# Written-out orders for TensorE, ScalarE and VectorE over the first part of an attention-and-MoE kernel, four masks moved to ScalarE, and shorter zero products

## The chip, the cores and the metric

One core of a Trainium2 chip runs the kernel. The metric is the device time of one execution in microseconds (us), the median of several runs. The engines are TensorE (PE; PEld is its weight load), VectorE (DVE), ScalarE (ACT), GpSimd (POOL), and the DMA queues, of which SyncE (SP) and POOL issue the ones that matter here.

## The reference

Three layers follow one another on 3072 tokens of 256 features (4 batches, 768 positions).

```python
# 1. a chunked linear attention with decay, 4 batches, 8 heads, width 32, state 16
log_a = np.log(np.clip(a, 1e-06, 1.0))
...
    L = np.exp(cum[:, :, :, None] - cum[:, :, None, :])
    L = L * causal
    CB = np.einsum('bhin,bhjn->bhij', Cc, Bc)
    M = CB * L
    y_intra = np.einsum('bhij,bhjd->bhid', M, xc)
    y_inter = np.einsum('bhin,bhnd->bhid', Cc, state) * decay_to_i[:, :, :, None]
    state = decay_full[:, :, None, None] * state + np.sum(Bx, axis=2)
# 2. a norm over the features and a gated layer, d_ff = 1536
rms = np.sqrt(np.mean(x * x, axis=-1, keepdims=True) + 1e-06)
xn = x / rms * rms_g
g = xn @ w_gate
silu = g * (1.0 / (1.0 + np.exp(-g)))
val = xn @ w_val
x = silu * val @ w_out
# 3. a second layer, d_ff = 2048
h = x @ w_in
g = h * np.clip(h + 3.0, 0.0, 6.0) / 6.0
out = g @ w_out
```

## The kernel before

The attention is cut into 24 chunks, numbered k, of 128 positions of one batch; chunks 4j to 4j+3 are one group of 512 tokens. Each chunk is worked in two halves of 64. The products of layers 2 and 3 are made from a high and a low part of each factor (names ending in h and l), as three products each.

Every piece of work is an operation of a planner (class `Plan`): it has a planned duration on one engine or more, keys that it reads and writes, and often a name (tag). `Plan.run` lays the operations out in planned time as a list scheduler does and then issues the instructions in that order. `P.chain(engine, names)` forces the named operations of an engine into the order given; what is not named goes where the planner puts it. Waits between the engines come from the data that the issued instructions touch. At the end `P.fill` looks at the planned time of TensorE between two named operations (`visit1` and `h010`) and puts zero products (`idle`, 128x256 in f32) into each gap that is longer than a product (430 ns) and `SLACK`.

The front is the work on the first 4 chunks. Its steps, with the names that the lists use (a number after a name is a chunk k, or a pair q of chunks):

- `heat`, `zero`, `warm`: products of zeros on TensorE. `sp`, `px` spread the decay over the partitions (bank tiles Q).
- `scan`: VectorE makes the decay matrix L of a chunk. `bh`, `ch`: VectorE scales B and C. `P`: ScalarE copies the prefix products out of PSUM.
- `sc`, `gr`: TensorE makes the scores and the state products of a chunk in a PSUM tile `sps`, one for chunks 0 and 1, another for 2 and 3.
- `SM`: VectorE multiplies scores and L. `um`: the state product times a mask of zeros and ones. `V`: VectorE makes the state at the end of the chunk.
- `visit0`, `visit1`: TensorE makes the attention's result of two chunks from `SM`, `um` and `ch` in the same `sps` tile.
- `sq`, `ev`: ScalarE squares and copies that result. `mn`: TensorE sums the squares. `rt` (ScalarE), `v`, `iv`, `nw` (VectorE): the inverse root. `bk`: TensorE spreads it. `sx`: VectorE scales. `xh` (ScalarE), `xl` (VectorE): high and low part of the normed input for layer 2.

After the front come the weights of layer 2, block f of 12: a load on SP's queue into one of six buffers, `wa` and `wb` (ScalarE), `wj` (VectorE; when it is done the buffer's next load can be issued), `wh` (high part, either engine) and `wl` (low part, VectorE).

Layer 2 itself runs in steps i: `h` (TensorE, hidden products; `h000` to `h111` are those of the first two blocks, cut into halves of 256 tokens and named by block, half, gate or value; from step 4 on they are `h4:0`, `h4:1`, ...), `s` (ScalarE, silu), `m` (VectorE, times the value), `g` (ScalarE, high part), `l` (VectorE, low part) and `r` (TensorE, the result). `h010` is the first product of the second half and needs `xl1`. The later chunks are visited between these steps (`visit2None`, `visit32`, ...: the pair that begins, the pair that ends). For them POOL issues loads of L, of `cb` (chunk data) and of P; the first of these is held back by a one-element copy (`hold`, L499) that reads the result of `nw0`.

Products after the front are recorded under line L970 (function `mm3`), most VectorE products under L289 (`two`).

## Time and profile before

| | |
|---|---|
| median of 3 runs | 596.59 us (595.4 to 598.26) |
| the profiled execution | 595.57 us |
| its span, first to last instruction | 593.8 us |
| TensorE, weight load, VectorE, ScalarE, GpSimd busy | 585.7, 474.0, 471.7, 370.9, 35.5 us |
| granted TensorE clock over the span | 0.998 |

Times within the profile are counted from the first instruction. Matmuls are pipelined and their recorded durations overlap, so that what a product costs in a row of products is the distance between two starts; the same holds for the other engines, where a next instruction can start shortly before the recorded end of the one ahead. A row of the timeline merges neighbouring instructions of one kind (xN).

### The profile page before, as it was taken

The page shows a single profiled execution, that of the slowest core. Times are in us where ns is not written, and L with a number is a line of the kernel's source. Part 1 is how long each engine was busy: PE and PEld are TensorE (multiplying, and loading weights), DVE is VectorE, ACT ScalarE, POOL GpSimd, SP SyncE. Part 2 cuts the span into 40 slices and gives each one's busy share as a digit, 9 for nine tenths or more (in the row PEclk, how much of TensorE's full clock was granted, in tenths as well). Part 3 has the DMA queues.
Part 4 walks back from the last instruction along what each step waited for, and adds up shares of the span by engine and source line. Part 5 has one row for each costly group of instructions (what it writes and reads, how often), then busy time and mean ns, then how long its engine had stood idle before and what let it go on. Part 6 is the DMA issues. An engine that isn't in the chain of part 4 may idle for free.

```text
span 593.8 us, 10861 instructions
## 1 busy us (share of the span) xinstructions
PE 585.7 (99%) x4352; PEld 474.0 (80%) x4352; DVE 471.7 (79%) x870; ACT 370.9 (62%) x654; POOL 35.5 (6%) x64
## 2 busy tenths in 40 slices
PE   9999999999999999999999999999999999999997
PEld 6787878788778778877787778888888888888885
DVE  8999967947885597899999898787975759775665
ACT  3898523323433363677767787777876668776663
POOL 2403013003210000000000000000000000000000
PEclk9999999999999999999999999999999999999999
DMA  8996104305430111022020101200000000100001
GB/s 329 352 316 179 48 22 143 116 9 150 128 128 19 43 49 63 8 72 71 1 71 2 71 2 71 72 1 1 36 36 1 0 1 1 72 0 1 0 1 71
DMA packets 11130, 40.90 MB, mean 69 GB/s; under 512 B 2484, under 2 KB 3208, under 8 KB 10056
## 3 DMA queue, kind: packets, MB, share of 16 engines
q1 hardware_dynamic: 6312, 23.25, 10.8%
q0 software_dynamic: 4000, 15.74, 9.0%
q10 hardware_dynamic: 768, 1.22, 0.6%
q8 instruction: 34, 0.56, 0.4%
q14 instruction: 16, 0.13, 0.1%
HBM read 36.84 MB, written 3.35 MB: 68 GB/s over the span
## 4 chain that ended last, share of the span: by engine, by line
PE 85%; DVE 8%; DMA 3%; ACT 2%; issue 1%; ACTq 0%; DVEq 0%; SPq 0%
PE hps L970 57%; PE acc L970 23%; PE sps L588 1%; DVE unit L289 1%; PE sps L562 1%; DVE st L289 1%; DMA cb<-comb 1%; PE sps L598 1%; DMA raw<-w 1%; DVE gl L289 1%; DMA rb<-rnd 1%; DVE p L289 1%; PE sps L573 1%; DVE w1t L289 0%; DVE raw L1209 0%
## 5 line engine op out<-in xcount | busy, mean ns | idle before, releaser
L970 PE MATMUL hps<-xh,w1t 128*128 128x512 f32 (+1 forms) x544 | 146.5, 387 | 0.3 <-ACT p L999 0.2
L970 PEld LDWEIGHTS hps<-xh,w1t 128*128 128x128 f32 x544 | 99.4, 188 | 22.3 <-ACT unit L1472 0.8
L970 PE MATMUL hps<-xl,w1t 128*128 128x512 f32 (+1 forms) x380 | 108.9, 385 | 0.0
L970 PE MATMUL hps<-unit,w1t 128*128 128x512 f32 x324 | 90.2, 389 | 0.0
L970 PE MATMUL acc<-gh,w1t 128*128 128x512 f32 (+1 forms) x288 | 87.9, 387 | 0.0
L970 PEld LDWEIGHTS hps<-xl,w1t 128*128 128x128 f32 x380 | 70.8, 188 | 14.5
L970 PEld LDWEIGHTS hps<-unit,w1t 128*128 128x128 f32 x324 | 60.8, 188 | 12.7
L289 DVE TENSOR_TENSOR gl<-p,gh 128x512 fp32r<-128x512 f32 (+1 forms) x86 | 57.6, 674 | 13.3 <-ACT gh L1007 7.0
L970 PEld LDWEIGHTS acc<-gh,w1t 128*128 128x128 f32 x288 | 53.0, 188 | 11.3 <-issue 0.6
L1007 ACT CAST gh<-p 128x512 fp32r<-128x512 f32 (+1 forms) x50 | 30.2, 605 | 49.2 <-PE acc L970 48.6
L970 PE MATMUL acc<-gl,w1t 128*128 128x512 f32 (+1 forms) x158 | 60.7, 384 | 0.0
L1314 ACT ACTIVATE p<-hps,half 128x512 f32<-128x512 f32 x48 | 33.0, 688 | 34.2 <-PE hps L970 34.1
L289 DVE TENSOR_TENSOR unit<-hps,unit 128x512 f32<-128x512 f32 x36 | 24.8, 689 | 35.6 <-PE hps L970 35.6
L999 ACT ACTIVATE p<-hps 128x512 f32<-128x512 f32 (+1 forms) x50 | 29.0, 579 | 36.6 <-DVE gl L289 22.5
L1003 DVE TENSOR_TENSOR p<-p,hps 128x512 f32<-128x512 f32 (+1 forms) x50 | 33.0, 660 | 22.3 <-PE hps L970 20.3
L970 PE MATMUL acc<-unit,w1t 128*128 128x512 f32 x142 | 42.8, 390 | 0.0
L1317 DVE SCALAR_TENSOR_TENSOR p<-p,hps 128x512 f32<-128x512 f32 x48 | 32.9, 686 | 10.8 <-ACT p L1314 10.5
L1321 ACT CAST unit<-p 128x512 fp32r<-128x512 f32 x48 | 29.6, 620 | 8.9 <-DVE p L1317 7.4
L1314 ACT ACTIVATE p<-unit,half 128x512 f32<-128x512 f32 x48 | 34.6, 720 | 0.9 <-DVE unit L289 0.4
L970 PEld LDWEIGHTS acc<-gl,w1t 128*128 128x128 f32 x158 | 29.7, 188 | 6.1
L1321 ACT CAST gh<-p 128x512 fp32r<-128x512 f32 x48 | 29.5, 619 | 7.2 <-DVE p L1317 6.4
L1317 DVE SCALAR_TENSOR_TENSOR p<-p,unit 128x512 f32<-128x512 f32 x48 | 33.0, 689 | 0.8 <-ACT p L1314 0.3
(185 smaller groups left out, 960.6 us busy)
## 6 DMA issues: line engine op xcount, KB each, us to landing
cb<-comb POOLq DMA_DIRECT2D x10, 896.0 KB, 5.6
raw<-w SPq DMA_DIRECT2D x8, 1024.0 KB, 4.8
L<-azero POOLq DMA_DIRECT2D x20, 256.0 KB, 4.5
yT<-w SPq DMA_DIRECT2D x6, 768.0 KB, 8.5
rawx<-w SPq DMA_DIRECT2D x6, 768.0 KB, 9.7
out<-yT SPq DMA_DIRECT2D x10, 256.0 KB, 2.0
P<-pref POOLq DMA_DIRECT2D x20, 64.0 KB, 2.5
rb<-rnd SPq DMA_DIRECT2D x5, 256.0 KB, 3.0
```

The lines of the kernel that those rows point to most:

```text
L289: eng[e].tensor_tensor(out=out, in0=a, in1=b, op=op)
L562: pe.matmul(out=o[64 * c:64 * c + 64, p ^ c], lhsT=cb[r, BN + c * SC:BN + (c + 1) * SC], rhs=cb[r, CP + c * CH:CP + (c + 1) * CH], start=T ...
L573: m = pe.matmul(out=o[32 * p:32 * p + 32, c], lhsT=b[r, s:s + 32], rhs=cb[r, XX + 64 * p:XX + 64 * p + 64], start=False, stop=True, skip_g ...
L588: pe.matmul(out=part(k, Y)[32 * g:32 * g + 32, 2 * t + c], rhs=T["SM", k][r, h ^ 2 * c], lhsT=T["cb", k][r, XX + D * h:XX + D * h + D], st ...
L598: ms.append(pe.matmul(out=y[u % 2 * 64:u % 2 * 64 + 64, u // 2 * 2 + n], lhsT=before(k, c)[r, :], rhs=T["ch", k][r, SC * n:SC * n + SC], s ...
L970: pe.matmul(out=o, lhsT=a, rhs=c, start=first and i == 0, stop=last and i == len(seq) - 1, skip_group_check=skip)
L999: act.activation(out=p[:, :n], in_=hcols(0), func=AF.Silu)
L1003: dve.tensor_tensor(out=p, in0=p, in1=hcols(1), op=ALU.mult)
L1007: act.copy(out=t[:, :n], in_=T["p", i][:, :n])
L1314: act.activation(out=unit(pk), in_=h(), func=AF.Relu, scale=1.0 / 6.0, bias=half)
L1317: dve.scalar_tensor_tensor(out=unit(pk), in0=unit(pk), scalar=1.0, in1=h(), op0=ALU.min, op1=ALU.mult)
L1321: P.op({"ACT": a1(512) + 20}, lambda e: act.copy(out=unit(gk), in_=unit(pk)), r=[pk], w=[gk])
```

## The change

- The written orders of TensorE, ScalarE and VectorE are replaced. The old lists end at `h101`, `xh11` and `xl1`; the new ones go on to `h14:0`, `s13` and `m13`, that is through the whole first group of 512 tokens of layer 2. Many operations get a name for it, and nothing else.
- The masks `um0` to `um3` (four VectorE instructions, one for each chunk) become `um0` and `um2`, one operation for each pair of chunks, on ScalarE (two instructions each, Copy with a scale for each partition), as those of chunks 4 to 7 were already. `um0` is planned after the start of `SM0`.
- `zero` and `warm` are 256 columns and not 512. `SLACK` is 450 and not 150 ns.
- `wh0` goes from ScalarE to VectorE, `wh1` stays on ScalarE, `wh2` stays on VectorE (by the lists).
- `guess`, the first step of the inverse root of the later groups, is one VectorE instruction and not two.
- Some planned durations are changed (`v`, `iv`, `nw`, `bk`, `warm`, `zero`), which only the planner reads.

```diff
-    SLACK, BIAS = 150, 600
+    SLACK, BIAS = 450, 600
...
     def warm(e):
-        pe.matmul(out=T["ps", 0][:, 0], lhsT=zero, rhs=four(zero), start=True, stop=True)
+        pe.matmul(out=T["ps", 0][:, 0, :256], lhsT=zero, rhs=four(zero, 2), start=True, stop=True)
...
-        P.op({"PE": 800}, lambda e: pe.matmul(out=Q[0], lhsT=zero, rhs=four(zero), start=True,
+        P.op({"PE": 430}, lambda e: pe.matmul(out=Q[0][:, :256], lhsT=zero, rhs=four(zero, 2), start=True,
                                               stop=True), w=[("z", 0)], tag="zero")
...
-        if k < B or last:
+        if last:
             P.op({"DVE": d1(64 * n)}, mask, r=[("Su", k // 2, k % 2), ("cs", 0)],
-                 w=[("um", k)] + ([("V1", k)] if k < B else []), boost=bst, ps=held(k),
-                 tag=f"um{k}")
+                 w=[("um", k)], boost=bst, ps=held(k), tag=f"um{k}")
         elif k % 2 == 0:
-            P.op({"ACT": 2 * a1(128)} if k < 2 * B and UMA else {"DVE": d1(256)}, mask2, r=[("Su", k // 2, i) for i in range(2)] + [("cs", 0)],
-                 w=[("um", i) for i in ks], boost=bst, ps=held(k), tag=f"um{k}")
+            P.op({"ACT": 2 * a1(128)} if k < 2 * B else {"DVE": d1(256)}, mask2,
+                 r=[("Su", k // 2, i) for i in range(2)] + [("cs", 0)],
+                 w=[("um", i) for i in ks] + [("V1", i) for i in ks if k < B],
+                 boost=bst, ps=held(k), tag=f"um{k}",
+                 seq=[("SM", i) for i in ks[:1] if k == 0])
...
     def guess(j, a, b):
         v, y, z = (t[:, a:b] for t in rn(j))
-        dve.tensor_scalar(out=z.bitcast(I32), in0=v.bitcast(I32), scalar1=1, scalar2=None,
-                          op0=ALU.logical_shift_right)
-        dve.tensor_scalar(out=y.bitcast(I32), in0=z.bitcast(I32), scalar1=-1.0,
+        dve.tensor_scalar(out=y.bitcast(I32), in0=v.bitcast(I32), scalar1=-0.5,
                           scalar2=float(0x5F3759DF), op0=ALU.mult, op1=ALU.add)
...
-    P.chain("DVE", "spot0 spot1 spot2 spot3 clip each prefix scan0 bh0 scan1 bh1 ch0 ch1 SM0 SM1 um0 "
-            "um1 scan2 scan3 bh2 bh3 ch2 ch3 wj0 v0 iv0 nw0 SM2 SM3 um2 um3 sx00 sx01 wl0 xl0 wj1 "
-            "v1 iv1 nw1 wj2 sx10 sx11 wl1 xl1")
-    P.chain("ACT", "P0 P1 wa0 wb0 sq0 sq1 wa1 rt0 ev0 ev1 wh0 wb1 wa2 xh00 xh01 sq2 sq3 wb2 rt1 ev2 ev3 "
-            "wh1 silu xh10 xh11")
-    P.chain("PE", "heat sp0 sp1 sc0 sc1 px gr0 gr1 sp2 sp3 visit0 zero mn0 mn1 sc2 sc3 gr2 gr3 bk0 warm visit1 "
-            "mn2 mn3 h000 bk1 h001 h100 h101")
+    P.chain("PE", "heat sp0 sp1 sc0 sc1 px sp2 gr0 gr1 sp3 visit0 zero sc3 sc2 gr3 gr2 mn0 mn1 bk0 warm "
+            "visit1 mn3 mn2 h000 bk1 h001 h100 h101 h010 h011 h110 h111 r0 h4:0 r1 h4:1 r2 visit2None "
+            "r3 h5:0 h5:1 r4 h6:0 h6:1 h7:0 h7:1 visit32 h8:0 r5 h8:1 r6 visitNone3 h9:0 h9:1 n1t "
+            "h10:0 h10:1 h11:0 r7 h11:1 r8 h12:0 h12:1 r9 h13:0 r10 h13:1 h14:0")
+    P.chain("ACT", "P0 P1 um0 wb0 wa0 sq0 sq1 wa1 wb1 rt0 ev0 ev1 um2 wa2 wh1 xh01 sq2 sq3 xh00 wb2 rt1 ev2 "
+            "ev3 silu xh11 s0 xh10 wb3 s1 g0 wb4 s2 g1 wa3 g2 s3 wa4 wa5 g3 wh3 s4 wb5 wh4 um4 g4 wb6 "
...
+    P.chain("DVE", "spot0 spot1 spot2 spot3 clip each prefix scan0 bh0 scan1 ch0 bh1 ch1 ch2 ch3 SM0 SM1 "
+            "scan2 scan3 V0 bh2 bh3 V1 wj0 SM2 SM3 v0 iv0 nw0 wj1 V2 wh0 sx01 sx00 wl1 wl0 xl0 v1 iv1 "
+            "nw1 wj2 V3 sx11 sx10 wh2 m0 xl1 wl2 m1 l0 scan5 m2 l1 scan4 m3 l2 wj3 wj4 bh4 l3 wl3 ch4 "
+            "m4 wj5 wl4 l4 U4 SM4 m5 wl5 wj6 scan7 m6 scan6 U5 bh6 V4 wj7 V5 wl6 m7 l5 wl7 U6 U7 V6 "
...
```

## Rows read from the trace of the kernel before

**Rows 1.** Windows, busy time of each engine; last columns: granted clock, DMA share, GB/s
```profile
9.39:25.71 16.32, 15.22 (x305) 11.72 (x289) 15.86 (x41) 13.13 (x27) 5.23 (x9) 1.00 1.03 374
25.71:590.00 564.29, 562.52 (x3978) 457.13 (x3978) 448.14 (x807) 355.48 (x624) 26.80 (x43) 1.00 0.17 55
```

**Rows 2.** Timeline of TensorE, from the first visit to the first product of the second half
```profile
11.40 0.86 PE L588 MATMUL sps<-SM,cb 64*32 64x64 f32 x64
...
21.07 0.73 PE L970 MATMUL hps<-xh,w1t 128*128 128x256 f32 x4
...
21.86 1.46 PE L390 MATMUL acc<-zero 128*128 128x256 f32 x6
23.16 0.61 PE L756 MATMUL sps<-eye,y 128*128 128x128 f32 x4
...
26.26 0.64 PE L970 MATMUL hps<-xh,w1t 128*128 128x256 f32 x4
...
26.98 0.28 PE L970 MATMUL hps<-xh,w1t 128*128 128x256 f32 x1
```

**Rows 3.** Timeline of VectorE over the same stretch
```profile
9.39 0.36 DVE L289 TENSOR_TENSOR ch<-cb,P 128x64 f32<-128x64 f32 x2 [0.26 <-ACT P L293]
9.67 1.28 DVE L619 TENSOR_TENSOR SM<-sps,L 128x512 f32<-128x512 f32 x2
10.87 0.48 DVE L626 TENSOR_TENSOR um<-sps,gs 128x128 f32<-128x128 f32 x2
11.26 2.33 DVE L511 TENSOR_TENSOR_SCAN L<-spread,eye 128x512 f32<-128x512 f32 x2
13.51 0.47 DVE L289 TENSOR_TENSOR bh<-cb,L 128x128 f32<-128x128 f32 x2
...
14.16 0.95 DVE L892 SCALAR_TENSOR_TENSOR yT<-yT 128x768 int32<-128x768 int32 x1
15.03 0.47 DVE L634 SCALAR_TENSOR_TENSOR V<-um,P 128x64 f32<-128x64 f32 x2
15.42 0.15 DVE L744 TENSOR_SCALAR v<-sps 128x2 f32<-128x2 f32 x1
...
23.37 0.56 DVE L295 CAST w1t<-fold 128x768 fp32r<-128x768 f32 x1
23.88 0.87 DVE L761 SCALAR_TENSOR_TENSOR xT<-xT,gs,sps 128x256 f32<-128x256 f32 x2
24.67 0.95 DVE L289 TENSOR_TENSOR w1t<-yT,w1t 128x768 fp32r<-128x768 f32 x1
25.71 0.69 DVE L289 TENSOR_TENSOR xl<-xT,xh 128x512 fp32r<-128x512 f32 x1
26.32 0.41 DVE L1003 TENSOR_TENSOR p<-p,hps 128x256 f32<-128x256 f32 x1
26.65 0.95 DVE L289 TENSOR_TENSOR w1t<-fold,w1t 128x768 fp32r<-128x768 f32 x1
```

**Rows 4.** Timeline of ScalarE at the mask of chunks 6 and 7
```profile
48.39 0.63 ACT L648 ACTIVATE um<-sps,gs 128x128 f32<-128x128 f32 x2 [0.23 <-DVE SM L639]
```

**Rows 5.** Windows around TensorE's idle time before `bk0`, and at the end of the program
```profile
14.43:16.38 1.95, 1.00 (x65) 0.70 (x65) 1.84 (x9) 1.04 (x4) 0.09 (x1) 1.00 1.02 426
588.00:592.00 4.00, 1.93 (x9) 1.27 (x7) 2.14 (x4) 0.74 (x2) 0.00 (x0) 1.00 0.62 230
592.00:594.00 2.00, 0.00 (x0) 0.00 (x0) 0.00 (x0) 0.00 (x0) 0.00 (x0) 0.50 0.19 64
```

**Rows 6.** Timeline of GpSimd and of SyncE's queue: loads of L, loads of weights
```profile
16.83 1.23 POOL L461 DMA_DIRECT2D L<-azero  x2 [0.35 <-POOL L L499]
15.14 8.60 SPq L901 DMA_DIRECT2D yT<-w  x3
```

**Rows 7.** Those two loads of L: issue to landing
```profile
DMA to landing us min/median/max: 8.6/9.1/9.6
```

**Rows 8.** DMA issues on the page: KB of one, us to landing
```profile
yT<-w SPq DMA_DIRECT2D x6, 768.0 KB, 8.5
```

## The prediction

> **What bounds the kernel now.** I read the windows first [rows 1]. From 25.71 us to 590.00 TensorE is busy for 562.52 of 564.29 us: all that its waits can still give back in this whole stretch is 1.77 us. In the front, from 9.39 to 25.71, VectorE is busy for 15.86 of 16.32 us and TensorE for 15.22, but a part of the latter is zero products. So the end of the program is set by the moment from which TensorE has products of layer 2 without a break, and that moment is set by VectorE. The products after it are the same in both kernels.

> The timeline of TensorE [rows 2] shows where that moment is. `h000` begins at 21.07, then come three zero products, `bk1` at 23.16, `h001`, two zero products, `h100`, which needs `wl1` (24.67 and 0.95 long [rows 3]), `h101` at 26.26 and `h010` at 26.98. A hidden product of 256 columns is six records, 0.72 us in all (26.26 to 26.98). From `h010` on the row is dense. `h010` needs `xl1`, and `xl1` begins at 25.71 and takes 0.69 [rows 3]. I therefore follow VectorE's queue from `ch0` (9.39, where it has waited 0.26 for ScalarE's `P0`, which the change leaves where it is) to `xl1`.

> **The change part by part: VectorE's queue.** The costs are distances between starts [rows 3].

> - Four masks leave: two in a row cost 11.26 - 10.87 = 0.39, so four 0.78. Gain.
> - `bh1` used to run while VectorE waited for `P0`; now it stands behind `ch0`. Two `bh` cost 13.89 - 13.51 = 0.38 with the `ch` at 13.89 following, one 0.19. Loss.
> - `wh0` comes from ScalarE. The cast at 23.37 is the same form, and 23.88 - 23.37 = 0.51. Loss.
> - `m0` now stands ahead of `xl1`: 26.65 - 26.32 = 0.33. Loss.
> - `SM0` must wait for `gr1`, and TensorE now makes `sp2` ahead of it. `sp2` is four records of 128x256 in f32; six such records of zeros took 23.16 - 21.86 = 1.30 [rows 2], so four 0.87. Before, `gr1` was done at about 9.6 (`SM0` began at 9.67). Now that is 10.5. VectorE arrives at 9.39 + 0.19 + four `ch` at 0.14 (0.28 for two, 9.39 to 9.67) = 10.14. Wait 0.37. Loss.
> - The old waits of the stretch: 16.32 - 15.86 = 0.46 idle [rows 1]. Some 0.2 of it lies between the short dependent instructions of the two inverse roots and stays; 0.26 goes. Gain.

> Sum: -0.78 + 0.19 + 0.51 + 0.33 + 0.37 - 0.26 = +0.36. `xl1` begins at 26.07 and ends at 26.76, later than before. Yet `h010` can follow at 26.8, since `wl1` and `wl0` are now both ahead of `xl0`, so that the four products `h000` to `h101` (2.88 us and `bk1`) no longer wait for `wl1` in the middle; they run from about 22.4 to 25.9. Against 26.98 the dense stretch begins 0.2 us sooner. The bounds: none of the 0.26 goes and the covers named below fail by 0.3 each, 0.9 us worse; `SM0` waits for nothing, 0.4 us better.

> **The masks on ScalarE, the norm, the zero products.** ScalarE's mask of a pair takes 0.63, and it was held until VectorE's `SM` of the same PSUM tile had ended (48.39, 0.23 of waiting) [rows 4]. I assume `um0` behind `SM1`: `SM0` at 10.5, two `SM` at 0.60 each end at 11.8, `um0` ends at 12.4, `visit0` begins there and not at 11.40. This one microsecond is hidden, because VectorE has 5 us of other work: two `SM` 1.2, two `scan` 2.25, `V0`, `bh2`, `bh3`, `V1` 0.78, `wj0` 0.87, `SM2` and `SM3` 1.2, and comes to `v0` at 16.8. TensorE's way there is the same work as before between 11.40 and its idle time ahead of `bk0`, which began at 14.43 + 1.00 = 15.43 [rows 2, 5], 4.03 us, less 0.43 for the shorter `zero`: `mn` ends at 16.0 and leaves 0.8 for ScalarE's root. That cover costs 0 while it holds. At `v1` and at `sx11` I estimate a cover of 0.3 each, laid end to end in the same way. The shorter `zero` and `warm` and the fewer `idle` give TensorE 0.4 us each, in a stretch in which it waits for VectorE anyway; I cost them at 0. The second instruction of `guess` saves VectorE 0.26 at each of the later norms, off the path, as TensorE is dense there: 0.

> **Behind `h010`.** TensorE comes to `h4:0` after four products and `r0`, 26.8 + 2.88 + 0.72 = 30.4. It needs `m2`, which frees a bank: VectorE goes from `xl1` (0.61), `wl2` 0.87, `m1` and `l0` 0.33 each to `scan5` at 28.2, 1.13, then `m2`, done at 29.75. The cover is 0.65.

> Behind `scan5` stands all of VectorE's queue, and `scan5` needs the load of L. It is two loads, issued when the held copy has seen `nw0`, at 16.83 and about 17.5 [rows 6]; they land 8.6 and 9.6 us after issue [rows 7], at 25.4 and 27.1. From `v0` (15.42) to the first issue 1.4 us pass; with `v0` at 16.8 the issue is at 18.2, so that L lands 1.4 later, at 28.5, and `scan5` waits 0.3, which the 0.65 covers. There is a second effect. `wj1`, behind which the load of weight block 7 is issued (the second of the three from 15.14 on [rows 6]), stood behind two `SM`, two `um`, `V2`, two `sx`, `wl0` and `xl0` after `nw0`, 4.1 us by the costs above, and now stands right behind `nw0`; with `nw0` 1.4 later it is issued some 2.7 us sooner, beside L. Its 768 KB [rows 8] at the 374 GB/s of the stretch [rows 1] are 2.1 us. Bounds for L: 28.5 if it costs L nothing, 30.6 if all of it goes ahead. I take 28.5, as the load issued at 15.14 was already ahead of L and L still came in 9 us; the other end is a rival.

> So the forecast is 0.2 us less: 595.4 for the profiled execution's own 595.57 (span 593.8 and 1.8 around it). The profiled execution lies 1.0 under the median of the runs, 596.59, and I state the time against the median: 596.4.

> **Rivals.**

> 1. The zero products were what held TensorE. Then `h000` stays at 21.07 and its three followers and `bk1` (0.45) run at once: `h010` at 21.07 + 2.88 + 0.45 = 24.4, 2.6 us sooner, 594.0. For it: three zeros stand between `h000` and `bk1`. Against it: `xl1` is behind a VectorE queue with 0.46 us of idle time in 16.32. 10%.

> 2. L is late. It decides from a landing at 28.85 on; each microsecond beyond holds `scan5`, `m2` and with them `h4:0`. At 30.6 that is 1.75, less the 0.2: 1.5 slower, 598.1. For it: the DMA engines' share is 1.03 in the front, there is nothing to spare. 18%.

> 3. `um0` is issued between `SM0` and `SM1`: the change plans it after the start of `SM0`, no more. Then `SM1` waits for `um0`: 0.69 + 0.63 + 0.05 in place of 0.60, and all of VectorE's queue is 0.77 later, with `h010` at 27.6: 0.6 slower, 597.2. For it [rows 4]: two engines don't read that tile together. 12%.
> [...]

> 4. The clock falls. [...] In the new order `mn1` ends at about 16.0 and `bk0` waits for `nw0`, which ends some 0.8 us after `v0` (the 1.4 above less the copy and its 0.35 of waiting), at 17.6: 1.6 us idle, with fewer and shorter zeros around it. If the clock falls there and is still down at 22.4, the four products take 5.8 us and not 2.9, `bk1` 0.9: `h010` at 29.0, 2.2 later: 598.6. 10%.
> [...]

> 5. The planner draws the rest of the program anew, since its planned times have changed. The most that it can give back is the 1.77 us of waits [rows 1]; it can lose as much. 594.8 or 598.2, 6% together.

> That the change does not do what it says is part of the forecast: the lists move much and the dense stretch begins where it began.

> **How the numbers follow.** The forecast, 44%, has its own range from 595.3 to 597.4, by the bounds of the sum above (0.4 better, 0.9 worse) and the spread of the runs (595.4 to 598.26). Rivals 2 to 4 and half of 5 lie above it, 43%, 1 and the other half of 5 below it, 13%. The range from 594.2 to 598.9 leaves out the lower half of rival 1 and the upper third of rival 4, and what both L late and the clock would do together. About 0.5%, 3 us, is what a measurement of this kernel can tell from no change. Faster by more needs rival 1 with a lucky rest, or several of the gains that I cost at 0: 8%. Slower by more needs rival 4 or 2 with another loss: 9%. The rest, 83%, is the same.

> **What would show it.** `um` on ScalarE behind `SM1` and `visit0` near 12.4; `SM0` near 10.5 with a wait for `gr`; `v0` near 16.8 with no wait; `h000` near 22.4, `h010` near 26.8; no idle VectorE at `scan5` beyond 0.3; the clock at 1.00. The prediction is wrong in its step if `xl1` begins well before 26 (then VectorE's queue had other slack than I see), if `h4:0` or `r4` waits for VectorE, or if the gain or loss lies behind 60 us.

## The result, and the profile after

The changed kernel takes 601.69 us, median of 6 runs (599.62 to 603.25), beside 597.07 of the kernel before (6 runs). The ratio is 1.0083, 95% interval [1.0064, 1.0102]: 4.6 us or 0.8% slower. I had forecast 596.4 and a range up to 598.9, and had given "slower by over 0.5%" 9%: the forecast was wrong. The profiled execution took 602.80 us, its span is 600.9.

The windows say where to look. The first stretch goes from `ch0` to `h010`, the second from there on.

```profile
9.57:33.24 23.67, 17.45 (x319) 14.00 (x317) 17.57 (x42) 13.93 (x30) 7.26 (x11) 0.78 0.91 317
33.24:597.00 563.76, 561.42 (x3970) 456.00 (x3968) 447.04 (x802) 352.31 (x620) 26.85 (x41) 1.00 0.17 53
```

Before, `h010` began at 26.98 [rows 2]; now it begins at 33.24, 6.3 us later of the 7.1 by which the span grew. Behind it TensorE is dense as before (561.42 of 563.76). In the front TensorE and VectorE are each idle for 6 us, where before they had 1.10 and 0.46 [rows 1], and the granted clock is 0.78. The timeline of TensorE in that front, with lines left out:

```profile
12.87 0.86 PE L587 MATMUL sps<-SM,cb 64*32 64x64 f32 x64 [1.13 <-ACT um L645]
...
15.34 0.33 PE L572 MATMUL sps<-cb,bh 64*32 64x64 f32 x13
18.76 0.41 PE L572 MATMUL sps<-cb,bh 64*32 64x64 f32 x19 [3.09 <-issue]
19.10 1.87 PE L712 MATMUL sps<-ones,sq 128*128 128x1 f32 x8
22.27 1.20 PE L755 MATMUL sps<-eye,y 128*128 128x128 f32 x4 [1.30 <-ACT xT L292]
...
27.61 0.72 PE L970 MATMUL hps<-xh,w1t 128*128 128x256 f32 x4
```

TensorE stops for 3.09 us in the middle of `gr3` and `gr2`, after 13 of 32 records of one form, and the view names no releaser ("issue"). Their neighbours in the same tile had just run, so late data are unlikely; the third step below tests it. Then `mn` takes 1.87 us, and 1.30 us of waiting follow before `bk0`. In the kernel before the same eight records of `mn` took 0.98, and the 32 records of `gr` ran in one row:

```profile
13.45 0.98 PE L711 MATMUL sps<-ones,sq 128*128 128x1 f32 x8
...
14.98 0.45 PE L573 MATMUL sps<-cb,bh 64*32 64x64 f32 x32
```

VectorE follows TensorE:

```profile
10.81 1.29 DVE L618 TENSOR_TENSOR SM<-sps,L 128x512 f32<-128x512 f32 x2 [0.41 <-PE sps L572]
...
19.23 1.29 DVE L618 TENSOR_TENSOR SM<-sps,L 128x512 f32<-128x512 f32 x2 [3.24 <-PE sps L572]
21.30 0.16 DVE L743 TENSOR_SCALAR v<-sps 128x2 f32<-128x2 f32 x1 [0.78 <-ACT z L747]
```

The granted clock (third value from the end) in the stop and in the three stretches behind it:

```profile
15.67:18.76 3.09, 0.00 (x1) 0.00 (x0) 0.32 (x1) 0.89 (x2) 0.00 (x0) 1.00 1.04 427
19.10:25.80 6.70, 5.40 (x98) 4.42 (x94) 4.98 (x13) 3.35 (x8) 3.31 (x5) 0.50 0.63 225
25.90:29.30 3.40, 2.76 (x18) 2.18 (x19) 2.85 (x9) 3.03 (x8) 2.46 (x5) 1.00 0.94 256
29.40:32.70 3.30, 3.30 (x17) 3.30 (x17) 2.98 (x8) 2.81 (x6) 1.39 (x2) 0.50 1.00 303
```

TensorE does nothing in the stop, and just behind it the clock is at 0.50 for most of the way to `h010`. Up to `visit0` the front went much as forecast: the mask on ScalarE begins at 12.19, behind `SM1`:

```profile
12.19 0.62 ACT L645 ACTIVATE um<-sps,gs 128x128 f32<-128x128 f32 x2 [2.48 <-PE spread L404]
```

What had TensorE waited for in the stop? The page counts the transfers by kind. Besides the data there are 34 packets of kind "instruction" on one queue, 0.56 MB, and TensorE's records are 4340 products and as many weight loads:

```profile
PE 587.2 (98%) x4340; PEld 475.3 (79%) x4340; DVE 471.9 (79%) x865; ACT 368.6 (61%) x654; POOL 37.6 (6%) x64
...
q8 instruction: 34, 0.56, 0.4%
```

That is 8680 records to 34 packets, 255 for each, which fits packets of TensorE's own instructions; the experiments test it. The view of the DMA queues in short windows tells when one goes. In the kernel before, the first goes between 12.2 and 13.2 (begun at 12.32):

```profile
q1 hardware_dynamic: 169, 0.39, 99.2%
q8 instruction: 1, 0.02, 6.1%
```

In the changed kernel the same window has none, and the first goes between 16.4 and 17.4 (begun at 16.47), 2.3 us before TensorE goes on:

```profile
q1 hardware_dynamic: 71, 0.42, 103.7%
q8 instruction: 1, 0.02, 5.8%
```

Up to there TensorE has begun 443 records:

```profile
0.00:18.70 18.70, 13.17 (x221) 8.46 (x222) 12.89 (x35) 6.28 (x12) 3.46 (x12) 1.00 0.91 348
```

### The profile page after: what moved, and what is told of

Its sections match the earlier page's. It is cut to its first block, busy times and chain, and to the rows that moved or that the text cites. A ratio compares the mean times of both kernels' runs of the same rounds, so it can differ in the third digit from the quotient of the medians.

```text
span 600.9 us, 10824 instructions
## 1 busy us (share of the span) xinstructions
PE 587.2 (98%) x4340; PEld 475.3 (79%) x4340; DVE 471.9 (79%) x865; ACT 368.6 (61%) x654; POOL 37.6 (6%) x64
## 4 chain that ended last, share of the span: by engine, by line
PE 91%; DVE 3%; DMA 2%; ACT 2%; issue 1%; ACTq 0%; DVEq 0%; SPq 0%
PE hps L970 61%; PE acc L970 23%; PE sps L587 2%; PE sps L561 1%; PE sps L597 1%; DMA cb<-comb 1%; DMA rb<-rnd 1%; PE sps L572 1%; DVE unit L288 1%; PE sps L712 0%; DVE raw L1209 0%; PE sps L755 0%; PE spread L404 0%; PE sps L811 0%; DVE st L288 0%
## 5 line engine op out<-in xcount | busy, mean ns | idle before, releaser
L970 PEld LDWEIGHTS hps<-unit,w1t 128*128 128x128 f32 x324 | 60.8, 188 | 12.7
L288 DVE TENSOR_TENSOR gl<-p,gh 128x512 fp32r<-128x512 f32 (+1 forms) x86 | 57.6, 673 | 14.2 <-ACT gh L1007 8.0
L970 PEld LDWEIGHTS acc<-gh,w1t 128*128 128x128 f32 x288 | 53.1, 188 | 11.2 <-issue 0.4
L1314 ACT ACTIVATE p<-hps,half 128x512 f32<-128x512 f32 x48 | 33.1, 689 | 34.1 <-PE hps L970 34.1
L999 ACT ACTIVATE p<-hps 128x512 f32<-128x512 f32 (+1 forms) x50 | 29.0, 580 | 35.0 <-PE hps L970 17.4
L1003 DVE TENSOR_TENSOR p<-p,hps 128x512 f32<-128x512 f32 (+1 forms) x50 | 33.1, 661 | 21.8 <-PE hps L970 18.5
L1317 DVE SCALAR_TENSOR_TENSOR p<-p,hps 128x512 f32<-128x512 f32 x48 | 32.9, 685 | 10.7 <-ACT p L1314 10.5
L1321 ACT CAST gh<-p 128x512 fp32r<-128x512 f32 x48 | 29.5, 619 | 7.2 <-DVE p L1317 6.4
```

The lines of the kernel that those rows point to most:

```text
L288: eng[e].tensor_tensor(out=out, in0=a, in1=b, op=op)
L970: pe.matmul(out=o, lhsT=a, rhs=c, start=first and i == 0, stop=last and i == len(seq) - 1, skip_group_check=skip)
L999: act.activation(out=p[:, :n], in_=hcols(0), func=AF.Silu)
L1003: dve.tensor_tensor(out=p, in0=p, in1=hcols(1), op=ALU.mult)
L1314: act.activation(out=unit(pk), in_=h(), func=AF.Relu, scale=1.0 / 6.0, bias=half)
L1317: dve.scalar_tensor_tensor(out=unit(pk), in0=unit(pk), scalar=1.0, in1=h(), op0=ALU.min, op1=ALU.mult)
```

## The experiments

"Packet" is the start of the first packet of TensorE's instructions, "stop" TensorE's idle time without a releaser up to `h010`, "clock" the granted clock of the profiled span; these four are from one profiled execution for each kernel. A name that begins with "a" is the changed kernel with an edit, one with "b" the kernel before with an edit. Ratios are to the kernel before.

| kernel | packet | stop | `h010` | clock | ratio [95%] |
|---|---|---|---|---|---|
| before | 12.3 | 0 | 27.0 | 0.998 | 1 |
| after | 16.5 | 3.09 | 33.2 | 0.990 | 1.0083 [1.0064, 1.0102] |
| a_gr_first | 15.6 | 2.72 | 31.8 | 0.990 | 1.0055 [1.0033, 1.0076] |
| a_mn_first | 16.1 | 1.12 | 32.3 | 0.991 | 1.0060 [1.0039, 1.0081] |
| a_zeros | 15.5 | 1.68 | 30.8 | 0.997 | 1.0062 [1.0040, 1.0084] |
| b_sp2_first | 14.0 | 0.50 | 29.0 | 1.000 | 1.0013 [0.9998, 1.0029] |
| a_hold4 | 15.1 | 2.49 | 32.0 | 0.991 | 1.0055 [1.0033, 1.0076] |
| a_gr_hold4 | 15.6 | 2.54 | 32.3 | 0.991 | 1.0060 [1.0038, 1.0083] |
| a_hold_sq | 15.8 | 2.27 | 34.1 | 0.986 | 1.0072 [1.0058, 1.0087] |
| a_more | 12.6 | 0 | 30.1 | 0.991 | 1.0055 [1.0034, 1.0076] |
| a_fix | 14.2 | 1.36 | 32.1 | 0.988 | 1.0139 [1.0117, 1.0160] |
| a_fix_zeros | 13.4 | 0.56 | 29.5 | 0.997 | 1.0079 [1.0056, 1.0103] |
| b_um_act | 15.4 | 1.70, 4.07 | 36.1 | 0.994 | 1.0114 [1.0093, 1.0135] |
| a_um_dve | 13.8 | 0.24 | 28.1 | 0.997 | 1.0027 [1.0015, 1.0039] |
| a_one_wait | 14.1 | 0.47 | 30.4 | 0.991 | 1.0010 [0.9995, 1.0024] |
| b_one_wait | 13.3 | 0 | 28.4 | 0.999 | 0.9986 [0.9974, 0.9998] |
| a_um_dve_zeros | 13.7 | 0.73 | 29.4 | 0.997 | 1.0014 [1.0000, 1.0028] |
| b_zeros | 12.9 | 0.25, 0.78 | 27.0 | 1.000 | 0.9992 [0.9979, 1.0004] |
| a_best | 14.1 | 0 | 31.0 | 0.993 | 1.0020 [1.0005, 1.0036] |
| a_best_zeros | 14.4 | 0 | 30.5 | 1.000 | 1.0014 [1.0001, 1.0026] |

**First: which part of the new order.** a_gr_first puts `gr0 gr1` back ahead of `sp2`:

```diff
-px sp2 gr0 gr1 sp3
+px gr0 gr1 sp2 sp3
```

> The changed kernel with gr0 and gr1 back ahead of sp2 in TensorE's order, nothing else. Theory 1 (late instructions): TensorE's stop of 3.09 us in gr3/gr2, which no semaphore ends, is a wait for a packet of instructions; the packet is asked for at about TensorE's 150th record, which is in gr0/gr1, and the change moved that from 9.2 to 10.3 us, behind the third load of raw weights on SP's queue (9.27), so that the packet went at 16.47 instead of 12.32. Then here the packet goes near 12.5, no stop without a releaser is over 0.3 us up to h010, the granted clock stays at 1.00, h010 comes at 26.5 to 27.5, ratio 0.996 to 1.002 to the kernel before. Theory 2 (too many short products in a row: mn0 and mn1 no longer lie between visit0 and the 100 short products): the stop stays, ratio 1.006 to 1.010. Theory 3 (the clock falls for want of zero products): the clock still falls, 1.004 to 1.009.

a_mn_first puts `mn` back ahead of `sc3`:

```diff
-zero sc3 sc2 gr3 gr2 mn0 mn1 bk0
+zero mn0 mn1 sc3 sc2 gr3 gr2 bk0
```

> The changed kernel with mn0 and mn1 back ahead of sc3, sc2, gr3 and gr2 in TensorE's order, nothing else. Theory 1 (late instructions): the packet is still asked for behind the third load of raw weights and goes near 16.5; mn0 and mn1 run before the stop, which lies later in the program and is shorter (1.5 to 3 us) but ends at the same 18.7; SM2 waits until 19.2 as before, v0 comes a little sooner; h010 at 30 to 32.5, ratio 1.003 to 1.008. Theory 2 (too many short products in a row): the stop is gone, h010 near 27, ratio 0.998 to 1.002.

a_zeros has the old zero products, `warm` as `zero`:

```diff
-    SLACK, BIAS = 450, 600
+    SLACK, BIAS = 150, 600
...
-        pe.matmul(out=T["ps", 0][:, 0, :256], lhsT=zero, rhs=four(zero, 2), start=True, stop=True)
+        pe.matmul(out=T["ps", 0][:, 0], lhsT=zero, rhs=four(zero), start=True, stop=True)
```

> The changed kernel with the zero products of before: zero and warm of 512 columns, SLACK of 150 ns. Theory 3 (the clock falls for want of zero products, and that is the loss): the granted clock stays at 1.00 until the end, ratio 0.998 to 1.002. Theory 1 (late instructions): the stop of about 3 us with its packet near 16.5 stays, the clock falls behind it in any case, since the added products stand behind the stop; ratio 1.005 to 1.010.

b_sp2_first makes the opposite edit of a_gr_first in the kernel before:

> The kernel before with sp2 moved ahead of gr0 and gr1 in TensorE's order, nothing else. Theory 1 (late instructions): the packet is asked for about 1 us later, behind the third load of raw weights, and goes at 15 to 16.5 and not at 12.32; TensorE stops without a releaser for 2 to 3.5 us near 15.2, which is where its 450th record stands; ratio 1.004 to 1.010. Theory 2 (too many short products in a row): mn0 and mn1 still lie between, SM0 waits 0.4 us longer, nothing else; ratio 0.999 to 1.002.

In none of the three kinds of the changed kernel does the packet come early, so neither the place of `gr0`, nor that of `mn`, nor the zeros is why it is late; with `mn` first the stop is merely shorter and ends at about the same time (18.38). And in the kernel before `sp2` first does not make it late by more than 1.7 us, although `visit0` begins there at 12.71, nearly as late as in the changed kernel (12.87): a late `visit0` alone does not do it either. My theory 1 was wrong on what delays the packet, and its 150th record was a guess of mine that no run shows; whether TensorE waits for instructions at all is tested in the third step.

**Second: the queue.** Are weight loads ahead of the packet? a_hold4 holds the loads of blocks 4 and 5 until `um0` is done; a_gr_hold4 adds the order of a_gr_first; a_hold_sq, a run later, holds them until `sq1`:

```diff
-return (go, [("cb", 1, 1)]) if f == 3 else ()
+return (go, [("cb", 1, 1)]) if f == 3 else (late, [("sq", 0, 0), ("sq", 0, 1)]) if f == 4 else ()
```

> The changed kernel with the fourth of the early weight loads (block 4, and block 5 behind it on SP's queue) held until um0 is done, by a one-element GpSimd copy; TensorE's order is that of the change. In the runs so far the packet of instructions came at 12.32 (before), 13.98 (before with sp2 first) and 15.5 to 16.5 in all four kinds of the changed kernel, and TensorE stops at the 444th record where it has not come. Theory 1b: the packet is asked for in visit0, behind its wait for um0, and by then the loads of blocks 4 and 5, which sp3's end lets go at 11.8 and 12.2, are ahead of it. Then here the two loads go after 13.2, the packet goes before 14.3, no stop without a releaser over 0.3 us, clock 1.00, h010 at 26.5 to 27.8, ratio 0.997 to 1.002. Theory 1c: the packet is asked for earlier (in gr0 and gr1) and stands behind the load of block 3 or behind other traffic: it stays at 15 to 16.5, the stop stays at 1.5 to 3 us, ratio 1.005 to 1.009.

> The changed kernel with the held loads of blocks 4 and 5 and with gr0 and gr1 ahead of sp2. Theory 1b: as with the held loads alone, and visit0 at 12.4 in place of 12.9; h010 at 26 to 27.3, ratio 0.995 to 1.001. Theory 1c: packet near 15.6 and a stop of 1.5 to 3 us, ratio 1.004 to 1.008.

> The changed kernel with the loads of blocks 4 and 5 held until sq1 is done (about 14.3), by a one-element GpSimd copy, so that they can't be ahead of a request made in visit0 (the first such attempt let them go at 12.15, just as visit0 began). Theory 1b: packet at 12.8 to 14, stop under 0.3 us, ratio 1.001 to 1.005 (the clock may still fall before bk0). Theory 1d, or the traffic of block 3 and earlier: packet at 15 to 16.5, stop 1.5 to 3 us, ratio 1.005 to 1.009.

In a_hold4 the loads went at 12.15, as `visit0` began (12.19): it told nothing. In a_hold_sq they went at 15.0, and the packet still came at 15.76, with 2.27 us of stop:

```profile
12.90 0.86 PE L587 MATMUL sps<-SM,cb 64*32 64x64 f32 x64 [1.12 <-ACT um L645]
...
15.37 0.33 PE L572 MATMUL sps<-cb,bh 64*32 64x64 f32 x13
17.97 0.33 PE L572 MATMUL sps<-cb,bh 64*32 64x64 f32 x5 [2.27 <-issue]
```

Those two loads are not the reason.

**Third: the place in the stream.** a_more adds 16 small zero products between `sp1` and `sc0`, which shifts all later instructions by 64 records; a_fix adds 20, ahead of `sp3`, and a_fix_zeros the old zeros too:

```diff
-heat sp0 sp1 sc0 sc1 px sp2 gr0 gr1 sp3 visit0
+heat sp0 sp1 more sc0 sc1 px sp2 gr0 gr1 sp3 visit0
```

> The changed kernel with 16 more small products of zeros on TensorE (64 records of loads and products) between sp1 and sc0, where it waits for data; they change nothing but the place of every later instruction in the stream. Theory 1b: the instruction that asks for the packet now stands 64 records later in the stream than the products around it did, so the request falls into sp2 to sp3, ahead of visit0's wait and of the loads of blocks 4 and 5: packet at 11.5 to 13.5, no stop over 0.3 us, although the 444th record is now reached earlier in the program; h010 at 26.5 to 28, ratio 0.998 to 1.003. If the stop is not one of instructions but belongs to gr3 and gr2 (their data, or PSUM), it stays in the same product, 2 to 3 us, ratio 1.006 to 1.010.

> The changed kernel with 20 small products of zeros (80 records) between gr1 and sp3, spread over two banks so that they take about 0.5 us in a stretch in which TensorE waits for um0 anyway; they only shift later instructions in the stream. The request for the packet should fall into them, ahead of visit0's wait: packet at 11.5 to 13.7, no stop. Theory 4 (two causes: the late packet, and the clock that falls in the 1.3 us in which TensorE waits before bk0, as my fourth rival had it): bk0 at 17.8 to 18.5 behind 1.3 us idle, the granted clock still falls to 0.50 somewhere between 17 and 26, h010 at 28 to 29.5, ratio 1.002 to 1.005. Theory 1 alone (the packet was all): clock at 1.00, h010 at 27 to 27.8, ratio 0.998 to 1.002.

> The same, and the zero products of before (zero and warm of 512 columns, SLACK of 150 ns). Theory 4: with the stop gone the longer zeros around the 1.3 us before bk0 keep the clock at 1.00, or let it fall for under 3 us; h010 at 26.8 to 28.2, ratio 0.998 to 1.003. If the longer zeros make no difference to the clock: h010 at 28 to 29.5, ratio 1.002 to 1.005.

In a_more the packet went at 12.60, before `visit0` (13.76), and the stop was gone, in the same order of work on the same data: this shows that the stop is one of instructions.

```profile
13.76 0.86 PE L593 MATMUL sps<-SM,cb 64*32 64x64 f32 x64 [1.12 <-ACT um L651]
...
16.23 0.45 PE L578 MATMUL sps<-cb,bh 64*32 64x64 f32 x32
```

In time that gained little (1.0055 beside 1.0083, with intervals that overlap): the added products cost 0.9 us, the clock fell all the same behind the wait before `bk0`, and two new stops without a releaser came later, 0.96 us at 53.2 and 0.47 at 165.1. In a_fix three came, at 16.4, 55.5 and 168.4, two of them (1.65 and 1.66 us) in the dense part:

```profile
55.48 0.34 PE L605 MATMUL sps<-ch,V 32*64 32x64 f32 x7 [1.65 <-issue]
```

The packet that ends this stop goes at 53.1, and around its start the DMA engines were nearly idle (share 0.02, second value from the end):

```profile
50.00:53.80 3.80, 3.80 (x161) 3.00 (x160) 3.80 (x8) 3.12 (x5) 0.88 (x2) 1.00 0.02 4
```

TensorE goes on 2.4 us after the packet has begun, much as in the changed kernel (2.3). So full DMA engines are not needed for such a stop.

Moving the stream cures one boundary and spoils others, and my forecast for a_fix missed that. a_fix_zeros is another matter: its profiled execution has a single stop, of 0.56 us, and the kernel is still at 1.0079. There `h010` is 2.5 us late, and behind it TensorE waits for ScalarE for 1.05 us up to 288.56 and 0.95 up to 317.01, two waits that neither the kernel before nor the changed one has; what brought them was not traced.

**Fourth: one part alone.** b_um_act moves only the masks to ScalarE:

```diff
-SM0 SM1 um0 um1 scan2 ... SM2 SM3 um2 um3 sx00
+SM0 SM1 scan2 ... SM2 SM3 sx00
-P0 P1 wa0 ... rt0 ev0 ev1 wh0
+P0 P1 um0 wa0 ... rt0 ev0 ev1 um2 wh0
```

> The kernel before with one part of the change alone: the masks of the first four chunks on ScalarE, a pair at a time, um0 behind P1 and um2 behind ev1. All three written orders are otherwise those of before, so that mn0 and mn1 stay ahead of sc2. Theory 1b: visit0 waits for um0 until 12.0 to 12.5, the loads of blocks 4 and 5 go ahead of the packet, it goes at 14 to 16; TensorE reaches its 444th record near 16 and stops for 0 to 1.5 us; ratio 1.000 to 1.006. Theory 1c, or a cause in the new orders alone: packet at 12.3 to 13.5, no stop, ratio 0.997 to 1.002.

It is slower than the whole change. Two stops, in this timeline of TensorE:

```profile
17.68 0.44 PE L573 MATMUL sps<-cb,bh 64*32 64x64 f32 x27 [1.70 <-issue]
...
28.88 1.01 PE L972 MATMUL hps<-xh,w1t 128*128 128x256 f32 x4 [4.07 <-issue]
```

And the windows up to each of them count 443 and 697 records, 254 apart:

```profile
0.00:17.60 17.60, 13.92 (x221) 9.16 (x222) 13.53 (x40) 6.40 (x14) 4.37 (x15) 1.00 0.90 343
0.00:28.80 28.80, 21.00 (x348) 14.00 (x349) 20.64 (x56) 15.35 (x31) 10.14 (x23) 0.93 0.95 329
```

The view by line has a row for `visit0` in the changed kernel that the kernel before lacks: an instruction in TensorE's stream that only waits, done at 12.1.

```profile
L587 PEldq EVENT_SEMAPHORE  x1: 51/51/51, 12.1 to 12.1; - x1
```

With the mask on ScalarE `visit0` needs two engines, VectorE for `SM` and ScalarE for `um`, and the second wait became an instruction of its own; b_um_act has two of these, at 11.2 and 20.3, one ahead of each visit. a_um_dve puts the masks back on VectorE in the changed kernel (one wait):

```diff
-P0 P1 um0 wb0 ... SM0 SM1 scan2 ... SM2 SM3 v0
+P0 P1 wb0 ... SM0 SM1 um0 scan2 ... SM2 SM3 um2 v0
```

> The changed kernel with the masks of the first four chunks back on VectorE (a pair in one instruction, um0 behind SM1, um2 behind SM3). visit0 then waits for one semaphore and not for two, and starts at 12.4 to 12.7. Theory 1b (the loads of blocks 4 and 5 go ahead of the request): they are issued at 11.8 and 12.2 as before, packet at 15 to 16, stop 1.5 to 3 us, ratio 1.004 to 1.008. Theory 1d (the second wait, an instruction of its own in TensorE's stream, keeps the request back until it is over): packet at 12.3 to 14, stop under 0.5 us; ratio 1.000 to 1.004.

The packet came at 13.8 although `visit0` began at 12.56, hardly sooner than after the change, and 0.24 us of the stop were left:

```profile
12.56 0.86 PE L587 MATMUL sps<-SM,cb 64*32 64x64 f32 x64 [0.74 <-DVE um L649]
...
16.05 0.41 PE L572 MATMUL sps<-cb,bh 64*32 64x64 f32 x18 [0.24 <-issue]
```

**Fifth: the wait alone.** a_one_wait keeps the masks on ScalarE, and a small zero product with `SM1` ahead of `visit0` takes over its wait for VectorE; b_one_wait does that ahead of both visits in b_um_act:

```diff
+        if q == 0:
+            P.op({"PE": 60}, lambda e: pe.matmul(out=Q[0][:32, :64], lhsT=T["SM", 1][:64, 0, :32],
+                                                 rhs=zero[:64, :64], start=True, stop=True),
+                 r=[("SM", 1)], w=[("hot", 1)], tag="tick")
-sp3 visit0
+sp3 tick visit0
```

> The changed kernel, masks on ScalarE as in the change, with one small product of zeros and SM1 ahead of visit0: it takes over visit0's wait for VectorE, so that visit0's first instruction waits for ScalarE alone and no instruction that only waits stands in TensorE's stream there. visit0 starts when it did, near 12.9. Theory 1d (the separate waiting instruction keeps the packet back): packet at 13 to 14.4 in place of 16.47, stop under 0.6 us, SM2 at 16.5 to 17, bk0 near 18.2; the clock still falls behind the 1.3 us before bk0; h010 at 27.8 to 29, ratio 1.001 to 1.004. If it is the masks on ScalarE or the late visit0 itself: packet at 15 to 16.5, stop 2 to 3 us, ratio 1.006 to 1.009.

> The kernel before with the masks on ScalarE (which gave stops of 1.70 and 4.07 us and 1.0114), and such a small product ahead of visit0 and of visit1. Theory 1d: first packet at 12.3 to 14, second before 21, both stops under 0.6 us, ratio 0.997 to 1.003. If it is the masks on ScalarE as such: both stops stay, ratio 1.008 to 1.013.

```profile
12.35 0.29 PE L1107 MATMUL spread<-zero,SM 64*32 64x64 f32 x2 [0.41 <-DVE SM L618]
13.06 0.86 PE L587 MATMUL sps<-SM,cb 64*32 64x64 f32 x64 [0.41 <-ACT um L645]
...
16.33 0.41 PE L572 MATMUL sps<-cb,bh 64*32 64x64 f32 x20 [0.47 <-issue]
16.68 1.05 PE L712 MATMUL sps<-ones,sq 128*128 128x1 f32 x8
19.03 0.68 PE L755 MATMUL sps<-eye,y 128*128 128x128 f32 x4 [1.30 <-ACT xT L292]
```

`visit0` begins no sooner (13.06) and waits for the same two engines, yet the packet goes at 14.1 and the stop shrinks from 3.09 to 0.47 (the queue of instructions from 14.0 to 15.0):

```profile
q8 instruction: 1, 0.02, 6.0%
```

In b_one_wait neither stop is left; `gr` runs in one row, and `h000` follows without a wait:

```profile
16.02 0.45 PE L573 MATMUL sps<-cb,bh 64*32 64x64 f32 x32
...
22.46 0.72 PE L972 MATMUL hps<-xh,w1t 128*128 128x256 f32 x4
```

The ratio falls from 1.0083 to 1.0010, and from 1.0114 to 0.9986 in the kernel before: the separate waiting instruction is the cause of the late packet, and with it of most of the loss. These edits also move the later instructions in the stream, a_one_wait by three places (four records more, one wait less) and a_um_dve by one the other way. The packet is early in both and late between them, so the move alone does not explain it.

The place of the wait counts all the same. Ahead of `visit0` the changed kernel has 188 records:

```profile
0.00:12.80 12.80, 10.43 (x94) 6.61 (x94) 9.70 (x29) 2.53 (x7) 3.46 (x12) 1.00 0.86 316
```

The stop comes after the 443rd, and 443 less the 254 of one packet is 189: the wait stands where the records of one packet end and those of the next begin. In a_more the same wait stands 64 records further on, and there the packet goes (12.60) before the wait is over (13.08). That the start of the packet is tied to this boundary is argued from these counts, not measured.

**Sixth: the clock.** a_um_dve_zeros is a_um_dve with the old zeros; b_zeros is the kernel before with the new ones; a_best is a_one_wait with a product ahead of `visit1` too, `mn` ahead of `sc3`, and `v0 iv0 nw0` ahead of `wj0 SM2 SM3`; a_best_zeros has the old zeros as well. The lists of a_best:

```diff
-sp3 visit0 zero sc3 sc2 gr3 gr2 mn0 mn1 bk0 warm visit1
+sp3 tick0 visit0 zero mn0 mn1 sc3 sc2 gr3 gr2 bk0 warm tick1 visit1
...
-V1 wj0 SM2 SM3 v0 iv0 nw0 wj1
+V1 v0 iv0 nw0 wj0 SM2 SM3 wj1
```

> The changed kernel with the masks on VectorE (no stop worth the name, but a clock that fell for about 3 us, 1.0027) and the zero products of before. If the short zeros are what lets the clock fall: granted clock 1.00 or below it for under 1 us between 17 and 27, h010 at 26.8 to 27.8, ratio 0.998 to 1.002. If the 1.6 us of waiting before bk0 lets it fall in any case: h010 at 27.8 to 28.6, ratio 1.001 to 1.004.

> The kernel before with the zero products of the change alone (zero and warm of 256 columns, SLACK of 450 ns). No packet is late, so this is the clock alone. My forecast's view that the zeros cost nothing: clock at 1.00, h010 at 26.5 to 27.2, ratio 0.998 to 1.002. If they hold the clock around the 0.94 us before bk0: it falls to 0.50 for 3 to 7 us, h010 at 28 to 30, ratio 1.002 to 1.005.

> The changed kernel with both causes taken away: a small product with SM1 or SM3 ahead of visit0 and visit1 takes over one of their two waits (no late packet), and mn0, mn1 go ahead of sc3 and v0, iv0, nw0 ahead of wj0, SM2, SM3, as in the kernel before (no long wait of TensorE before bk0). Masks on ScalarE, shorter zeros and the later lists are those of the change. Theory 4 (late packet and clock are the whole loss): first packet at 13 to 14.3, no stop over 0.6 us, wait before bk0 at most 0.8 us, granted clock 1.00 from 7 us to the end, h010 at 26.8 to 28.4, ratio 0.996 to 1.000. If the change's lists cost something behind h010 too: 1.001 to 1.004 with the clock at 1.00.

> The same with the zero products of before. If the wait before bk0, and not the length of the zeros, decides on the clock: clock 1.00 in both, ratio within 0.002 of the other. If the short zeros count as well: the clock falls in the other kernel alone, and this one is 1 to 3 us faster.

In the profiled execution of b_zeros the clock stays up; over its 12 runs it was below 0.998 in 7, in the kernel before in 14 of the 35 beside it. The ratio, 0.9992, shows no cost of the short zeros in the old order. In a_um_dve_zeros the clock falls in all 12 runs in spite of the old zeros, in the profiled one behind 1.57 us of waiting for `bk0`. So there the longer zeros don't keep it up. And a_best, where that wait is gone, still has the clock at 0.50 from 15.7 to 22.5, and a_best_zeros does not (first a_best, then a_best_zeros); over the span it was below 0.998 in 11 of the 12 runs of a_best and in none of a_best_zeros:

```profile
15.70:22.50 6.80, 6.63 (x159) 5.14 (x158) 4.43 (x11) 4.29 (x9) 4.08 (x7) 0.50 1.00 384
```

```profile
15.70:22.50 6.80, 5.42 (x162) 3.71 (x162) 4.64 (x13) 4.41 (x9) 4.00 (x6) 1.00 0.95 368
```

In time the two are alike (1.0020 and 1.0014, and a_um_dve and a_um_dve_zeros overlap too). So the zeros are no large term, and my expectation that the wait before `bk0` alone decides on the clock was wrong.

What one fall is worth can be read from the kernel before itself. Of its 35 runs beside a_one_wait, 21 have a granted clock of 0.998 to 1.000 (median 596.50) and 14 one of 0.996 or 0.997 (median 598.27): 1.8 us.

The ratios mix these two kinds of runs, and two readings change when like is set beside like. b_one_wait has a clock of 0.998 or more in all of its 12 runs and takes 596.57, beside 596.50 of the 21: it is the one kernel with a ratio below 1 clear of noise, and it does the work no faster, its clock just did not fall. a_best_zeros has the clock up in all 12 as well and takes 598.18 (597.94 to 599.08), beside 596.43 (595.71 to 597.41) of the 10 such runs of the kernel before that were taken with it: 1.7 us slower, and not the 0.8 us of the ratio.

## Why the prediction was wrong, by its steps

**VectorE's queue up to `SM1`: right.** `SM0` waits 0.41 us for `gr1` (0.37 forecast) at 10.81 (10.5), `um0` on ScalarE comes behind `SM1` (12.19; `SM1` ends at 12.10), `visit0` at 12.87 (12.4). `ch0` was 0.18 late already. With that rival 3 fell: no `SM` was held by a mask, and what a mask issued between them would have cost was not tested.

**"TensorE's way there is the same work as before": the step that failed.** The work is the same, 4.03 us less 0.43, and the sum took it that TensorE has its instructions whenever it has its data. `mn` was to end at 16.0 and leave 0.8 us of cover; it ended at 20.97, 5.0 later. Of these the stop is 3.09, the half clock in `mn` about 0.9, the later `visit0` 0.5; the rest, 0.5, is spread over the row, 0.2 of it the shorter `zero`, which saved 0.21 and not 0.43 (13.96 to 14.71 now, 12.49 to 13.45 before). The cover took up part, and `v0` came at 21.30 instead of 16.8, 4.5 later. I costed moving the masks as VectorE's time against ScalarE's, and a hidden microsecond; its real price was a second wait ahead of `visit0`. Nothing in the rows of before shows that price, but the 34 packets of instructions on its page could have led to the question.

**Rival 4, the clock: it came, and I gave it too little.** TensorE waits 1.30 us before `bk0` (1.6 forecast) and the clock falls, but in the changed kernel it does so behind the stop. In a_one_wait, nearly without the stop, it falls too, and the ratio is still 1.0010. The rival's sum takes the four products at half the clock, 5.8 us and not 2.9: 0.50 is what the end of the kernel before shows [rows 5], and after the change three of them took 3.58 in place of 2.16. My price for it, 2.2 us, is of the size of the 1.8 above. Alone it was no reason for 0.8%.

**The zero products at 0:** no run contradicts it in the old order (b_zeros, 0.9992). In the new one the ratio moves by 0.06 to 0.21% with them in three pairs, whose intervals overlap. In the fourth, a_fix and a_fix_zeros, it moves by 0.6%, and there the two later stops of a_fix, 3.3 us in all, are gone too.

**From `v0` to `h010`:** forecast 10.0 us, measured 11.94. Of the 1.9 us, 1.4 are `h001`, `h100` and `h101` at the half clock (29.66 to 33.24, 3.58 where 2.16 was reckoned); the rest lies ahead of them and was not taken apart.

**Rival 2, L late: no.** The two loads of L that `scan5` needs land 6.9 and 7.4 us after issue (8.6 and 9.6 before [rows 7]); why sooner was not tested. VectorE begins `scan5` at 34.53 without a wait, and TensorE waits for nothing at `h4:0`. Rivals 1 and 3 did not come; behind `h010` (rival 5) TensorE's waits are 0.6 us more than before (2.34 beside 1.77).

**What stays open.** a_best_zeros has neither a stop nor a fall and is still above the kernel before, 0.14% by the ratio [1.0001, 1.0026] and 1.7 us with the clock up in both. In the profiled executions `h010` comes 3.5 us later than before and the span is 3.5 longer, so this cost of the new order lies in the front; `visit0` alone is 2.06 later (13.46). I did not trace it further. What lets the packet go, and what the 4.3 us ahead of it consist of, was not measured.

## What to carry to other kernels

Where TensorE runs many short instructions in a row, count its records to the next packet. In the front 254 records lasted 2.8 us (12.87 to 15.67), behind `h010` some 18 (7938 records in 563.76 us), and the long stops came in such short rows or just behind them. A second semaphore ahead of such a row can cost more than the work that the move saves: here 3.09 us of stop for the 0.78 of VectorE that the four masks took. An idle time that the profile puts to "issue" in the middle of equal instructions is to be held against the queue of kind "instruction" before anything else is explained by it. Let a cheap instruction just ahead, added if there is none, carry one of the two waits: in a_one_wait that left 0.47 of the 3.09 us.

## What the runs showed that I had not expected

- A second wait ahead of a visit cost TensorE 3.09 us of stop in the changed kernel, and two of them 5.8 us in b_um_act; a small product ahead of each visit took all of the latter back (1.0114 to 0.9986).
- 80 added records, which took 0.63 us (10.39 to 11.02), made the kernel 3.3 us slower than the change itself by the ratios (1.0139 to 1.0083). Its two stops at later boundaries of the stream, 1.65 and 1.66 us, are as much; the first came with the DMA engines nearly idle.
- The kernel before has a granted clock below 0.998 in 14 of 35 runs, which take 1.8 us more, close to half of its spread of 3.9 us.
